# Score products of two heads in two halves of the array's rows, with two-bank score tiles and one shared bank for projections and values

## The chip, the cores and the metric

The kernel runs on one core of a Trainium2 chip. The metric is the device time in microseconds of one execution, taken as the median of several runs; lower is better. The engines are named as in the profile: PE is TensorE's matmul queue, PEld its weight loads, DVE VectorE, ACT ScalarE, POOL GpSimd, SP SyncE, which issues the DMAs.

## The reference

One transformer block on x of shape (1, 2048, 512), with 32 heads of 16 and a window of 256 keys, all in fp32:

```python
sa, ca, ga, sb, cb, gb = split(silu(c) @ w_mod)
h = layernorm(x) * (1 + ca) + sa
x = x + ga * A(h, wqkv, wo)        # sliding-window attention
h = layernorm(x) * (1 + cb) + sb
x = x + gb * B(h, w1, w3, w2)      # silu(h@w1) * (h@w3) @ w2, width 1792

# in A:
scores = einsum("bhqd,bhkd->bhqk", q, k) * 16 ** -0.5
mask = (i - j >= 0) & (i - j < 256)
o = softmax(where(mask, scores, -1e9)) @ v
```

## The kernel before, in words

The program has three parts: a prologue (layer norm, modulation, values of all heads into `vS`), attention in 32 units, and the output projection with the feed-forward part. A unit is one group `g` of 4 heads and one block `b` of 512 queries (`g, b = divmod(u, NB)`, line 827 and its like). The 4 heads are two pairs, `a` = 0 and 1, with two heads `h` in each. Precision is kept by splitting fp32 operands into a rounded fp32r part and a remainder, so a product of two split operands takes three matmuls.

*Where the operands lie.* `ringk` holds keys and `ringq` queries, heads of a pair one above the other: head 0 in rows 0 to 47 (16 elements, three rows each for the split products), head 1 in rows 48 to 95. A query column has values in its own head's rows and zeros in the other's, so a product over all rows gives that head's scores alone. Rows 96 and 97 hold the negative maximum (rounded and remainder) in `ringq` and ones in `ringk`.

*The three steps of a unit.* `unit_a` (line 539): 12 matmuls of 128x128x512 project q and k into the bank `pj` (line 546), ACT copies it out twice (lines 554 and 557), POOL makes the remainder (561), and nine DMAs spread the rows into the rings (567, 569). `unit_b` (line 585): for each of 8 blocks of 64 queries and each pair, one matmul of 96 rows, 128 query columns and up to 320 keys gives scores in a bank `mx` (line 595, "bound product" in this text); DVE adds a mask and takes the row's maximum (604). A transpose on PE (610), a copy on ACT (614), the remainder on DVE (`low`, 617) and two DMAs (621) bring the maxima into rows 96 and 97. `unit_c` (line 825): scores again, with keys on the partitions (line 855), in tiles of one bank `st` with four slots of 128 columns. `WAYS` says for each of six tiles of a pair which key block meets which query blocks; one matmul covers both heads, so it has 256 columns for one query block and 512 for two. The diagonal block ("near") and the block at the window's far end ("far") hold complementary triangles. Where both of a key block's triangles are at hand, DVE merges the far one into the near one in PSUM (`copy_predicated`, 882; with no far block a mask is added, 884), ACT takes one exponential (892), and POOL splits the result into the two with zeros (`affine_select`, 865). Elsewhere ACT copies the block out (860), POOL masks it (865), and ACT takes the exponential (876). Then the value products (905): fp32, the probabilities moving, 17 weight columns (16 values and a one for the sum) of each of four heads into its own 32 partitions of the bank `po`; ACT copies `po` out (912), a DMA stores it (915).

*PSUM's eight banks.* `po` 1, `pj` 1, `mx` 3, `st` 3, all from the pool `psA` (lines 470 and 477). The prologue borrows `st` and `mx`; after attention, the planner of the feed-forward part uses all eight by the table `BANKS`.

*The order of the work.* It is written out. In attention each step has a time in the table `X`, in slots of which a unit has 8; steps of all units are sorted by it (line 1017) and issued in that order, each engine keeping it strictly. After the last units, `ORDER`, `ENGS` and `BANKS` give the order, the engine of each either-or step, and the bank of each product; `Y` and `W` order the prologue.

Of the kernel before, what the change touches and what calls it, by code (L numbers as in the profile page):

```python
# [8 lines left out]
F32 = mybir.dt.float32  # L9
# [9 lines left out]
P = 128  # L19
# [12 lines left out]
X = dict(wqk=(-20.0358, -11.9699, -7.5457), pj=(-28.4873, -28.2135, -28.0501, -27.4756, -25.9988, -25.9357,  # L32
         -25.6912, -25.4459, -24.706, -24.0099, -23.5356, -23.4491), ev=(-22.1624, -21.7023), mix=(-19.0403,),
         row=(-17.1032, -19.8185, -17.762, -16.6896, -19.2827, -20.0079, -16.268, -15.1151, -15.9758),
         mx=(-13.3225, -11.4955, -9.6326, -9.2616, -6.3262, -13.4791, -8.3568, -10.0235, -10.5657, -7.528,
         -7.4334, -11.8695, -7.9956, -6.5249, -9.9457, -11.8384), tl=(1.046, 0.61, 1.469, 1.173, 0.247, 0.052,
         0.282, 0.614, 0.93, 0.988, 1.257, 0.446, 0.598, 0.377, 0.675, 0.778), mr=(-5.806, -5.255, -4.853,
         -2.465, -2.209), st=(1.6653, 1.5726, -0.1141, -0.2946, -0.056, 0.9896, 4.7355, 5.3285, 3.1204, 2.6224,
         3.8659, 5.563), cp=(3.438, 88.47, 0, 0, 0, 0, 6.268, 5.867, 0, 0, 0, 0), mg=(0, 0, -0.004, 0, 0.342,
         1.791, 0, 0, 3.411, 0, 4.304, -58.918), sx=(2.609, 61.173, 0, -0.214, 0, -24.164, 4.963, 5.299, 0,  # L40
         2.956, 0, 5.662), ex=(8.23, 2.612, 0.733, 0, 0.811, 2.465, 9.686, 7.995, 4.324, 0, 4.933, 7.046),
         se=(6.102, -41.609, 1.394, 0, 5.111, 3.506, 9.147, 7.859, 9.091, 0, 8.301, 0.234), pv=(10.1765,
         10.1762, 10.1658, 10.1939, 10.1552, 10.1514), o=(14.1458, 19.2797), job=(3.4574, 10.7246, 14.4495),
         raw=-29.903, gate=18.537)
# [4 lines left out]
         0.331, 0.331, 0.331, 0.331, 0.119, 0.331, 0.331), mr=(8.547, 8.884, 8.95, 9.9, 10.016))  # L49
W = dict(m=0.18, s=0.307, a=0.29, t=0.562, p=0.366, vs=1.748, vo=0.433, wq=(-1.444, 1.47, 1.587), wv0=-2.239, wvh=(-0.578, -0.445, -0.399, -0.345), wvl=(-0.193, -0.326, -0.374, -0.317), wp=1, A0=2.112, h0=0.452, h=6.002, hb=6.868, ls=3.035, la=0.875, rf=(-1.1, -0.393, 6.445), v=2, vt=1.562, mr=(-1.837, 1.507), mm=(3.653, 5.841, 7.356, 7.655), ml=(-1.346, 1.651, 2.536, 6.904), A=1.465, At=7.897, B=10.563)  # L50
MODE = 'AB'
MXB = 3
STB = 3
XB = 6
PTB = 15
# [212 lines left out]
def us(t):  # L268
# [7 lines left out]
             job_dma=("SP", 0.5), scores=("PE", 0.19), top=("DVE", 0.5), parts=("DVE", 0.22), turn=("PE", 0.11), cut=("ACT", 0.16),  # L276
             rows=("SP", 0.67), probs=("ACT", 0.49), copy=("ACT", 0.48), merge=("DVE", 0.33), far=("PE", 0.125),
             part=("POOL", 0.73), part1=("POOL", 0.37), values=("PE", 0.43), cut_all=("ACT", 0.48), store=("SP", 0.45))
# [16 lines left out]
    "PPDDPDDDPDDDDPDPDDDDPPPPDPPDDPDPPPPDDPPPPDDDDDDDDDDPDDDPDDDPDDDDDPDPPPPDPDPDDPDDDDDPDDDDDPPPDDPDDPDD"  # L295
    "PPDPPDDDPPDDPDPPDPPDPPDDPPPPPPPPPPDDDPPPPPDDPPDDDPDDDPPPPPPPPPPPPPPPPDDDPPPDDDPPDDDDDDPDPPPDPPPPDDDP"
    "PDDDDPPPPPPDDDPPDDDDPPPPPPDDDPPDDDDPPPPPDPDDPPPPPPDDPPPPPDDDDDDDPPPPPPDDDPPDDDDPPPPPPDDDPPDDDDPPPPPP"
    "DDDPPDDDDPPPPPPDDDPPDDDDPPPPPPDDDPPDDDDPPPPPPDDDPPDDDDPP")
ORDER = (
# [102 lines left out]
BANKS = dict(dn=(  # L402
    "mpmmssosmmmpsomspmommssossmoommspsmmopmmmmsspmssssmomsmommopsmopspmsmsmsmmsssmssosmmmommpmssopssssmm"
    "psmmmmmosmmomsompsmsmsompsms"),
             tp=(
    "somsposm"),
# [1303 lines left out]
```

## Time and profile before

| | |
|---|---|
| median of 3 runs | 919.24 us (918.39 to 919.66) |
| profiled execution | 918.07 us, span 916.3 us |
| PE, PEld busy | 893.5, 726.0 us |
| DVE, ACT, POOL busy | 654.8, 513.6, 555.2 us |
| granted PE clock | 0.996 |

The span starts with the first instruction of the program and ends with the last. A group of instructions is written as: line, engine, operation, tiles (out<-in), shape, count, then the busy time, the mean of one, the idle time before the group, and what ended it. For a matmul "98x256" after "98*128" means 98 rows and 128 columns of weights, and 256 moving columns. Its recorded length holds the pipeline too, so the distance of two starts says better how long it keeps PE.

### The profile page before, as it was taken

What the parts mean: (1) busy time and instruction counts of PE and PEld (TensorE: products, weight loads), DVE (VectorE), ACT (ScalarE), POOL (GpSimd) and SP (SyncE); (2) the same over time, 40 slices, a digit from 0 to 9 for tenths busy, and PEclk for the clock granted to TensorE, in tenths of its full rate; (3) what the DMA queues carried; (4) which work ended last, traced back from release to release, by engine and by line L of the source; (5) the groups of instructions that cost most, each with busy time, mean ns of one, the idle gap of its engine ahead of it and who ended that gap; (6) DMA issues with size and microseconds to landing.
All of it is one profiled execution on the core that took longest, in us unless ns stands there. A gap on an engine that the chain in (4) does not pass through costs nothing.

```text
span 916.3 us, 18353 instructions
## 1 busy us (share of the span) xinstructions
PE 893.5 (98%) x6052; PEld 726.0 (79%) x6052; DVE 654.8 (71%) x1786; ACT 513.6 (56%) x962; POOL 555.2 (61%) x796
## 2 busy tenths in 40 slices
PE   6999999999999999989998999999999999999998
PEld 2688788888888888866776888888888888888886
DVE  7676778788887778786679668758568665565555
ACT  3433777778778777766597834343465334332330
POOL 6211687787888787867676356886569355435220
PEclk9999999999999999998999999999999999999999
DMA  9631456566655655567875677574272423231102
GB/s 330 201 93 36 109 158 171 165 173 171 178 161 165 174 159 156 144 170 220 266 224 184 211 245 247 174 235 145 85 264 65 159 76 104 66 100 43 46 24 93
DMA packets 126083, 141.73 MB, mean 155 GB/s; under 512 B 61090, under 2 KB 73890, under 8 KB 125988
## 3 DMA queue, kind: packets, MB, share of 16 engines
q1 hardware_dynamic: 125268, 139.51, 50.4%
q10 hardware_dynamic: 720, 1.05, 0.4%
q8 instruction: 48, 0.79, 0.4%
q14 instruction: 47, 0.39, 0.1%
HBM read 85.72 MB, written 34.61 MB: 131 GB/s over the span
## 4 chain that ended last, share of the span: by engine, by line
PE 85%; DMA 4%; DVE 4%; ACT 2%; POOL 2%; issue 2%; SPq 0%; ACTq 0%; POOLq 0%; DVEq 0%
PE st L1472 11%; PE mx L1472 10%; PE pj L548 9%; PE st L855 8%; PE po L905 8%; PE mx L595 7%; PE mx L1568 7%; PE st L1568 6%; PE st L759 5%; PE pj L1472 4%; PE po L1472 3%; PE po L1568 2%; PE pj L1568 2%; DMA vS<-in_wmod 1%; POOL pt L865 1%
## 5 line engine op out<-in xcount | busy, mean ns | idle before, releaser
L604 DVE CUSTOM_DVE_ANT_0 junk<-mx,mskq 128x320 bf16<-128x320 f32 (+4 forms) x512 | 216.5, 466 | 55.0 <-PE mx L595 53.0
L865 POOL TENSOR_SCALAR_AFFINE_SELECT pt<-pt 128x256 f32<-128x256 f32 x472 | 184.7, 413 | 65.9 <-ACT pt L892 26.4
L595 PE MATMUL mx<-ringk,ringq 96*128 96x320 f32 (+4 forms) x512 | 149.3, 314 | 1.6 <-DMA ringq<-qk 1.6
L548 PE MATMUL pj<-hT,wq 128*128 128x512 f32 x384 | 140.2, 401 | 0.0
L892 ACT ACTIVATE pt<-st 128x512 f32<-128x512 f32 (+1 forms) x216 | 117.3, 573 | 33.1 <-DVE st L882 27.6
L855 PE MATMUL st<-ringq,ringk 98*128 98x256 f32 (+1 forms) x536 | 128.4, 328 | 3.3 <-DMA ringq<-mT 1.9
L1067 POOL TENSOR_TENSOR w<-w,w 128x512 fp32r<-128x512 f32 (+2 forms) x49 | 85.2, 1754 | 55.9 <-ACT w L1066 55.2
L595 PEld LDWEIGHTS mx<-ringk,ringq 96*128 96x128 f32 x512 | 95.9, 190 | 13.5 <-issue 2.4
L855 PEld LDWEIGHTS st<-ringq,ringk 98*128 98x128 f32 x536 | 88.3, 191 | 13.3 <-issue 2.5
L905 PE MATMUL po<-pt,vS 128*17 128x128 f32 (+1 forms) x2144 | 89.0, 314 | 0.4 <-ACT pt L876 0.4
L548 PEld LDWEIGHTS pj<-hT,wq 128*128 128x128 f32 x384 | 71.6, 190 | 10.3
L905 PEld LDWEIGHTS po<-pt,vS 128*17 128x17 f32 x2144 | 60.8, 98 | 23.1 <-issue 5.1
L882 DVE COPY_PREDICATED st<-later,st 128x256 f32<-128x256 uint8 x152 | 62.0, 426 | 23.3 <-PE st L855 21.3
L1519 POOL TENSOR_TENSOR t<-t,t 128x512 f32<-128x512 f32 x25 | 33.5, 1342 | 65.4 <-DVE t L1507 65.4
L1472 PE MATMUL st<-b,w 128*128 128x512 f32 x270 | 67.0, 390 | 0.2 <-DVE x1a L1573 0.2
L1472 PEld LDWEIGHTS st<-b,w 128*128 128x128 f32 x270 | 50.5, 188 | 11.5 <-DVE x1a L1573 0.7
L876 ACT ACTIVATE pt<-pt 128x512 f32<-128x512 f32 (+1 forms) x96 | 52.6, 587 | 9.6 <-POOL pt L865 9.4
L860 ACT ACTIVATE pt<-st 128x512 f32<-128x512 f32 (+1 forms) x96 | 52.0, 546 | 8.8 <-PE st L855 8.1
L561 POOL TENSOR_TENSOR qk<-qkr,qk 128x512 fp32r<-128x512 f32 x32 | 41.5, 1298 | 20.0 <-ACT qk L557 19.8
L1066 ACT ACTIVATE w<-w 128x512 fp32r<-128x512 f32 (+2 forms) x56 | 42.4, 784 | 18.7 <-DMA w<-wraw 11.4
L1507 DVE TENSOR_TENSOR t<-mx,t 128x512 f32<-128x512 f32 x44 | 30.1, 685 | 29.4 <-ACT t L1514 12.5
L1507 DVE TENSOR_TENSOR t<-st,t 128x512 f32<-128x512 f32 x40 | 27.4, 686 | 26.7 <-ACT g L1495 9.3
(310 smaller groups left out, 1887.0 us busy)
## 6 DMA issues: line engine op xcount, KB each, us to landing
ringq<-qk SPq DMA_DIRECT2D x192, 64.0 KB, 2.1
ringk<-qk SPq DMA_DIRECT2D x96, 128.0 KB, 2.4
o_dr<-os SPq DMA_DIRECT2D x32, 256.0 KB, 2.2
w<-wsum SPq DMA_DIRECT2D x14, 512.0 KB, 4.3
w<-w2g SPq DMA_DIRECT2D x14, 512.0 KB, 3.7
jb<-in_w SPq DMA_DIRECT2D x24, 256.0 KB, 3.7
w<-wraw SPq DMA_DIRECT2D x14, 384.0 KB, 5.7
vS<-in_wmod SPq DMA_DIRECT2D x20, 256.0 KB, 5.0
```

The lines of the kernel that those rows point to most:

```text
L548: nc.tensor.matmul(v["ps"], WQ[g][w][:, n // 3], hTp(i, n // 3, b * BT, BT), start=(n == 0), stop=(n == 3 * KC - 1))
L595: nc.tensor.matmul(v[i][:, :n], both_queries(a, gs), keys(NS, a, (gs + 1) * HP - n, n), start=True, stop=True)
L604: nc.vector.tensor_tensor_reduce(out=junk[:, :n], in0=v[i][:, :n], in1=mskq[:, WK - n:], scale=1.0, scalar=-3e38, op0=ALU.add, op1=ALU.max ...
L855: nc.tensor.matmul(piece(v[a, k], a, k, m), keys(NM, a, kb * P, P), queries(a, 4 * b + q, n), start=new, stop=not new or len(here(a, k)) = ...
L865: nc.gpsimd.affine_select(out=out, in_=in_, **w)
L882: nc.vector.copy_predicated(o, later, block(v[a, fk], a, fk, m))
L892: nc.scalar.activation(o, i, AF.Exp, scale=SCALE)
L905: nc.tensor.matmul(po[32 * i:32 * i + DH + 1, q * P:(q + n) * P], vS[:, 4 * b + j, 4 * g + i], piece(pt_of(a, k), a, k, m)[:, h], start=i ...
L1067: either(lambda e: e.tensor_tensor(out=lo(), in0=src(), in1=hi().bitcast(F32), op=ALU.subtract), 0.85, 0.06 + 0.0024 * n, key, kl + kh, kl ...
L1472: nc.tensor.matmul(ps(bk), WT[s, n][w][:, col], BB[t, k][r], start=start and c == 0, stop=stop and c == 5, skip_group_check=True)
L1507: return nc.vector.tensor_add(o, x, y)
L1568: nc.tensor.matmul(ps(bk), tiles[hk + (h,)][:, i * P:(i + 1) * P], w2_of(last, y, f), start=(m == 0), stop=(m == 5))
```

## The change

- **Rows.** Each head of a pair gets 64 rows of its own (`HP` = 64): head 0 rows 0 to 63, head 1 rows 64 to 127, with the split's three rows interleaved at a stride of 4. The fourth row holds the negative maximum for the first of the 16 elements; all the rings' free rows are filled with zeros (`ringq`) and ones (`ringk`).
- **Score products.** One matmul of 98 rows for both heads becomes two of 64 rows, one for each head, with half the columns.
- **Score tiles.** Six tiles of one bank for each pair become three of two banks, one bank for each head, with four slots of 128 columns; two such tiles in place of three one-bank tiles. `PIECES` gives key block, first query block, count and slot. In each tile a near and a far block of one key block are merged, so there are six merges in a unit (five before); one block in each of the first two tiles is copied, masked and exponentiated by itself.
- **Maxima.** The bound product now reads all 128 rows, the old maximum of the group before among them, so its result is relative to that; a sum `mtb` for each query block is kept on DVE (`add`), rounded to fp32r. The step `low` goes, and one row is written for each head.
- **Banks.** `pj` and `po` become one bank, `pp`; the values write 32 rows of weights' columns for each head (the 17, and 15 more that lie behind them in memory). The prologue gets four banks of its own (`s0`), attention two two-bank tiles, the feed-forward part four single banks (`sd`), from three pools over the same four banks.
- **Tables.** New `X`, `ENGS`, `ORDER` and `BANKS`; the job's buffer is single; `W` is as before. In the new `X` a unit's PE work stands, by slot, in this order: score tile, bound product, projection, 2 bound, 2 projections, score tile, 2 bound, score tile, 2 bound, values, transpose, bound, score tile, 3 bound, score tile, 2 projections, bound, projection, score tile, bound, 2 projections, bound, 2 projections, bound, projection, bound, projection.

```diff
-STB = 3
+STB = 4
-PTB = 15
+PTB = 8
...
-    def queries(a, qb, n):
+    def queries(a, h, qb, n):
         b, i = divmod(qb, 4)
-        return ringq[:NM, b, a, 2 * i:2 * (i + n)].rearrange("p s h t -> p h s t")
+        return ringq[HP * h:HP * h + HP, b, a, 2 * i:2 * (i + n), h]
...
-    def keys(rows, a, lo, n):
-        return ringk[:rows, a, lo:lo + n]
+    def keys(a, h, lo, n):
+        return ringk[HP * h:HP * h + HP, a, lo:lo + n]
...
-                v["ps"] = psA.tile([P, BT], F32, name="pj", bufs=1)
+                v["ps"] = psA.tile([P, BT], F32, name="pp", bufs=1)
...
+        def add():
+            nc.vector.tensor_tensor(out=mtb[b], in0=v["mt"], in1=mtb[b].bitcast(F32), op=ALU.add)
...
-        def low():
-            nc.vector.scalar_tensor_tensor(out=v["mT"][:, 1], in0=v["tp"][:16, :P], scalar=-1.0,
-                                           in1=v["mT"].bitcast(F32)[:, 0], op0=ALU.mult, op1=ALU.subtract)
...
+    psD = psx.enter_context(tc.tile_pool(name="psD", bufs=1, space=PSUM))
+    PIECES = (((0, 0, 3, 0), (3, 3, 1, 3)), ((1, 1, 3, 1), (-2, 0, 1, 0)), ((2, 2, 2, 0), (-1, 0, 2, 2)))
+    NEAR, FAR, ONE = (0, 1, 0), (2, 3, 3), ((3, 0), (0, 1))
+    EXPS = ((0, 2), (1, 2), (0, 3))
...
+        def scores(a, n):
+            v[a, n] = psD.tile([P, 2, 4, P], F32, name="st", bufs=2)
+            does = here(n)
+            for m, (j, q, c, to) in enumerate(does):
+                for h in range(2):
+                    nc.tensor.matmul(v[a, n][:, h, to:to + c], keys(a, h, (4 * b + j) * P, P), queries(a, h, 4 * b + q, c),
+                                     start=m == 0, stop=m == len(does) - 1, skip_group_check=True)
...
+        def probs(a, n):
+            lo, c = EXPS[n]
+            if n == 2 and not b:
+                c = 2
+            nc.scalar.activation(pt_of(a, n)[:, lo:lo + c].rearrange("p n h k -> p h n k"), v[a, n][:, :, lo:lo + c],
+                                 AF.Exp, scale=SCALE)
...
+        def values_of(n):
+            if "po" not in v:
+                v["po"] = psA.tile([P, BT], F32, name="pp", bufs=1)
+            for j, q, c, at_ in here(n):
+                for i in range(4):
+                    nc.tensor.matmul(v["po"][32 * i:32 * i + 32, q * P:(q + c) * P],
+                                     vflat[:, at_v(4 * b + j, 4 * g + i):at_v(4 * b + j, 4 * g + i) + 32],
+                                     pt_of(i // 2, n)[:, at_:at_ + c, i % 2], start=i not in first, stop=False,
+                                     skip_group_check=True)
+                    first.append(i)
```

More of the change, by code (lines that the diff above doesn't have):

```diff
@@ L275 @@
 KINDS = dict(product=("PE", 0.235), mix=("POOL", 1.25), qk_rows=("SP", 0.65), out=("ACT", 0.5), job=("POOL", 2.0),
-             job_dma=("SP", 0.5), scores=("PE", 0.19), top=("DVE", 0.5), parts=("DVE", 0.22), turn=("PE", 0.11), cut=("ACT", 0.16),
+             job_dma=("SP", 0.5), scores=("PE", 0.28), top=("DVE", 0.5), parts=("DVE", 0.22), turn=("PE", 0.11), cut=("ACT", 0.16),
              rows=("SP", 0.67), probs=("ACT", 0.49), copy=("ACT", 0.48), merge=("DVE", 0.33), far=("PE", 0.125),
-             part=("POOL", 0.73), part1=("POOL", 0.37), values=("PE", 0.43), cut_all=("ACT", 0.48), store=("SP", 0.45))
+             part=("POOL", 0.73), part1=("POOL", 0.37), values=("PE", 0.85), cut_all=("ACT", 0.48), store=("SP", 0.45))
 NPE = 3
@@ L865, in window, with merge @@
             nc.gpsimd.affine_select(out=out, in_=in_, **w)
[L867 to L882 removed]
+        def merge(a, n):
+            o = v[a, n][:, :, NEAR[n]]
+            if n < 2 or b:
+                nc.vector.copy_predicated(o, later, v[a, n][:, :, FAR[n]])
@@ L900, in values_of @@
-        def values_of(k):
-            for a in range(2):
-                for m, (j, q, n) in enumerate(here(a, k)):
-                    for h in range(2):
-                        i = 2 * a + h
-                        nc.tensor.matmul(po[32 * i:32 * i + DH + 1, q * P:(q + n) * P], vS[:, 4 * b + j, 4 * g + i],
-                                         piece(pt_of(a, k), a, k, m)[:, h], start=i not in first, stop=False,
-                                         skip_group_check=True)
-                        first.append(i)
+        def probs(a, n):
[4 more added lines that the diff above has]
+                                 AF.Exp, scale=SCALE)
@@ new lines, in part, with copy, mask, masked_probs @@
+        def part(a, n):
+            pt = pt_of(a, n)
+            window(pt[:, FAR[n]], pt[:, NEAR[n]], 1, 0.0)
+            window(pt[:, NEAR[n]], pt[:, NEAR[n]], 0, 0.0)
+        def copy(a, n):
+            i = ONE[n][0]
+            nc.scalar.activation(pt_of(a, n)[:, i], v[a, n][:, :, i], AF.Copy)
+        def mask(a, n):
+            i, far = ONE[n]
+            window(pt_of(a, n)[:, i], pt_of(a, n)[:, i], far, NEG)
+        def masked_probs(a, n):
+            o = pt_of(a, n)[:, ONE[n][0]]
+            nc.scalar.activation(o, o, AF.Exp, scale=SCALE)
@@ L920, in unit_c @@
         for a in range(2):
-            for k in range(6):
-                i = 6 * a + k
-                does = here(a, k)
-                for m in range(len(does)):
-                    put("sx" if m else "st", i, "scores" if does[m][2] == 2 else "far", scores, a, k, m)
-                if not does or k == 3:
-                    continue
-                if k == 0 or k == 1 and len(WAYS[MODE[a]][k]) == 2:
-                    put("cp", i, "copy", copy, a, k)
-                    put("se", i, "part" if len(does) > 1 else "part1", mask, a, k)
-                    put("ex", i, "probs", masked_probs, a, k)
-                else:
-                    if k in FAR[MODE[a]]:
-                        put("mg", i, "merge", merge, a, k)
-                        if here(a, FAR[MODE[a]][k][0]):
-                            put("se", i, "part", part, a, k)
-                    put("ex", i, "probs", probs, a, k)
-        for k in range(6):
-            if here(0, k) + here(1, k):
-                put("pv", k, "values", values_of, k)
+            for n in range(3):
+                i = 3 * a + n
+                put("st", i, "scores", scores, a, n)
+                put("mg", i, "merge", merge, a, n)
+                put("ex", i, "probs", probs, a, n)
+                if n < 2 or b:
+                    put("se", i, "part", part, a, n)
+                if n == 0 or n == 1 and b:
+                    put("cp", i, "copy", copy, a, n)
+                    put("s2", i, "part1", mask, a, n)
+                    put("e2", i, "probs", masked_probs, a, n)
+        for n in range(3):
+            put("pv", n, "values", values_of, n)
         at(t0 + X["o"][0], out, "cut_all")
@@ L1021, in block_kernel, with singles, take @@
     fixed = [(us(t), fn, *KINDS[kind]) for t, _, fn, kind in last]
-    names = [("st", STB)] * 3 + [("mx", MXB)] * 3 + [("pj", 1), ("po", 1)]
-    free = [end - 1.0] * 3 + [us(8 * (NU - 1) + X["mr"][1]) + 0.4] * 3 + [0.0, end]
+    names = [("sd", STB)] * 4 + [("mx", MXB)] * 3 + [("pp", 1)]
+    free = [end - 1.0] * 4 + [us(8 * (NU - 1) + X["mr"][1]) + 0.4] * 3 + [end]
     urgent = [us(t) for t, _, _, kind in last if kind in ("rows", "qk_rows")]
     ids = {-1 - o[1]: o[2] for o in last}
-    sch = Sched(free, lambda i: psA.tile([P, BT], F32, name=names[i][0], bufs=names[i][1]), fixed, urgent)
     pools = {"a1": a1}
+    def singles():
+        psx.close()
+        pools["sd"] = ctx.enter_context(tc.tile_pool(name="psE", bufs=1, space=PSUM))
+    def take(i):
+        if i < STB and "sd" not in pools:
+            singles()
+        pool = pools["sd"] if i < STB else psA
+        return pool.tile([P, BT], F32, name=names[i][0], bufs=names[i][1])
+    sch = Sched(free, take, fixed, urgent)
     def ps(b):
@@ L1657, in block_kernel @@
             for b in o.bank:
-                b.tile = (sch.take, dict(s=0, m=3, p=6, o=7)[BANKS[b.use][b.n]])
+                b.tile = (sch.take, dict(s=0, m=4, p=7)[BANKS[b.use][b.n]])
     else:
```

160 lines of the change are left out of this document (57 added, 103 removed), and 202 rows, old and new, of the table ORDER.

## The prediction

> **What bounds the kernel now.** I read the page first: its engine line and the chain that ended last.
>
> ```profile
> span 916.3 us, 18353 instructions
> PE 893.5 (98%) x6052; PEld 726.0 (79%) x6052; DVE 654.8 (71%) x1786; ACT 513.6 (56%) x962; POOL 555.2 (61%) x796
> ...
> PE 85%; DMA 4%; DVE 4%; ACT 2%; POOL 2%; issue 2%; SPq 0%; ACTq 0%; POOLq 0%; DVEq 0%
> ```
>
> PE is busy for 98% and is 85% of the chain. The profiled execution took 918.07 us, 1.8 us more than its span; the median of the three timed runs, 919.24, lies 1.2 us above it. I make the sum in span time and add its result to the median.
>
> A mean over the span hides stages, so next I took three windows: attention in its steady state, its end, and the feed-forward part. After that I asked for PE's waits in the first window, and for the transpose of the maxima (line 610), which occurs once in each unit.
>
> ```profile
> 150.00:400.00 250.00, 249.82 (x2643) 211.04 (x2633) 201.47 (x895) 192.97 (x399) 201.12 (x425) 1.00 0.59 164
> 400.00:500.00 100.00, 91.19 (x619) 67.33 (x619) 75.54 (x171) 71.68 (x141) 68.83 (x86) 0.97 0.73 217
> 500.00:916.00 416.00, 412.01 (x1831) 340.46 (x1830) 270.04 (x369) 171.54 (x273) 214.85 (x156) 1.00 0.41 133
> ...
> PE mx L595 <- DMA ringq<-qk: 0.2, 1, 0.2
> ...
> L610 PE MATMUL mx<-ident,mt x23: 276/277/280, 150.2 to 384.8; 128*16 128x128 f32 x23
> ```
>
> Columns of the windows: stretch, length, then PE, PEld, DVE, ACT, POOL. In the first window PE waited 0.2 us in 250. So a nanosecond taken from PE there is a nanosecond of the kernel, until another engine fills up. The 23 transposes have 22 periods between 150.2 and 384.8, so a unit takes 10.66 us. DVE has 201.47/250 x 10.66 = 8.59 us of work in a unit, POOL 8.58, ACT 8.23. The slack before the next engine binds is about 2 us a unit. The last window holds no score product; its tables change but not its products, and I cost it at nothing, +-1 us.
>
> "Busy" counts each matmul's pipeline as well, so I price products by the distance from one start to the next. The timeline of PE alone, around one unit's value products:
>
> ```profile
> 310.25 0.30 PE L905 MATMUL po<-pt,vS 128*17 128x128 f32 x4
> 310.48 0.28 PE L610 MATMUL mx<-ident,mt 128*16 128x128 f32 x1
> 310.51 0.39 PE L595 MATMUL mx<-ringk,ringq 96*128 96x320 f32 x1
> 310.74 0.28 PE L855 MATMUL st<-ringq,ringk 98*128 98x256 f32 x1
> 310.86 0.31 PE L595 MATMUL mx<-ringk,ringq 96*128 96x320 f32 x1
> ...
> 316.76 0.40 PE L548 MATMUL pj<-hT,wq 128*128 128x512 f32 x1
> 317.00 0.31 PE L595 MATMUL mx<-ringk,ringq 96*128 96x320 f32 x1
> 317.15 0.40 PE L548 MATMUL pj<-hT,wq 128*128 128x512 f32 x1
> ...
> 317.54 0.40 PE L855 MATMUL st<-ringq,ringk 98*128 98x512 f32 x1
> 317.78 0.31 PE L595 MATMUL mx<-ringk,ringq 96*128 96x320 f32 x1
> ...
> 318.28 0.31 PE L595 MATMUL mx<-ringk,ringq 96*128 96x320 f32 x1
> 318.52 2.15 PE L905 MATMUL po<-pt,vS 128*17 128x256 f32 x52
> ```
>
> A projection of 512 columns occupies PE for 0.24 us (316.76 to 317.00), a bound product of 320 for 0.15 (317.00 to 317.15), a score product of 256 for 0.12 (310.74 to 310.86) and of 512 for 0.24 (317.54 to 317.78). Going between products of 96, 98 and 128 rows costs nothing. At the values it is different: the bound product before them holds PE for 0.24 (318.28 to 318.52), 0.09 too much.
>
> **Part by part: the score products.** Their groups, over the whole run, by shape, and the value products of the unit above:
>
> ```profile
> L855 PE MATMUL st<-ringq,ringk 98*128 98x256 f32 x352 | 74.4, 290 | 2.5 <-DMA ringq<-mT 1.9 <-ACT pt L892 0.7
> L855 PE MATMUL st<-ringq,ringk 98*128 98x512 f32 x184 | 68.6, 403 | 0.8 <-ACT pt L892 0.8
> ...
> L905 PE MATMUL po<-pt,vS x52: 272/273/391, 318.5 to 320.4; 128*17 128x128 f32 x32, 128*17 128x256 f32 x20
> ```
>
> Now: 352 x 0.12 + 184 x 0.24 = 86.4 us of PE. The change makes 704 products in 352 pairs (24 units with 6 pieces for each of 2 head pairs, 8 first units with 4). The columns are as many as before, but the two products of a pair lie in different halves of the rows and write different banks. If a pair runs side by side, its time is that of one product, and 43.2 us go. If not, nothing goes. No pair of row halves is in this trace. The nearest row is the value products: the 52 above are 13 groups of four heads in four 32-column strips, 8 groups of 128 columns and 5 of 256, or 18 steps of 128. Their starts reach from 318.5 to 320.4, 0.11 us a step, a quarter of what they would take one after the other. So products in separate parts of the array do overlap here, fully, and I take the 43.2. The Trainium skill, "TensorE: Matmul & The Clock Gate", section "Measured speedup vs the span model", has a measured speedup of 3.07 for four row strips; if two strips kept the same share (an estimate, 1.53), about 30 us would go instead, and my sum would end near 903.
>
> **Going between tilings.** All six score tiles of a unit stand alone in the new table, each with full-height products on both sides: 192 tiles, 384 borders. What a border costs is the dispute of this prediction. The low end is zero, as between 96, 98 and 128 rows. The high end is the border of the values: 0.09 on the way in; on the way out the last group of four starts at 310.25 and the next product at 310.48, 0.23, or 0.12 over a step; then the first 128-column weights are not there ahead, and the bound product from 310.51 to 310.74 takes 0.23 instead of 0.15, 0.08 more. In, out and 0.08 for the weights each way are 0.37 us a tile. I take zero, since the row that keeps all 128 columns and varies only the rows is nearer than the one that narrows the columns to 17; the other end is a rival below.
>
> **One bank for q/k and values.** Now a projection waits for two copies of ACT, then the values take the bank, then a third copy, then the next projection.
>
> ```profile
> 318.27 0.58 ACT L554 ACTIVATE qkr<-pj 128x512 f32<-128x512 f32 x1
> 318.75 0.59 ACT L557 ACTIVATE qk<-pj 128x512 fp32r<-128x512 f32 x1
> ...
> 320.92 0.27 ACT L614 ACTIVATE mT<-mx 16x128 fp32r<-16x128 f32 x1 [0.82 <-PE mx L610]
> ...
> 324.39 0.59 ACT L912 ACTIVATE os<-po 128x512 f32<-128x512 f32 x1
> ```
>
> The pair of copies takes 1.07 us (318.27 to 319.34), and starts only when the last projection's record ends, 0.40 after its start: 1.47 from start to free. In the new table two score tiles and four bound products stand between: 0.24 + 2 x 0.24 + 4 x 0.15 = 1.32. PE is late by about 0.2 a unit, all of PE's work queued behind it. On the other side the copy of 0.59 (and the small one of 0.27 ahead of it) has two tiles and four bound products as cover, 1.1 us: nothing, or 0.1. I take 0.2 x 32 = 6 us; its bounds are 0 (the copies start at once, and PE is slower there than I think) and 10.
>
> **Two score tiles in flight instead of three.** Per unit six two-bank tiles replace twelve one-bank tiles. Five of six have 2 us of PE work or more until their buffer is wanted again. The tile of the second pair's middle piece has only about 1.6 (tile, three bound products, three projections and again a bound one), while its own chain is merge, exp and a copy:
>
> ```profile
> L882 DVE COPY_PREDICATED st<-later,st 128x256 f32<-128x256 uint8 x152 | 62.0, 426 | 23.3 <-PE st L855 21.3
> L892 ACT ACTIVATE pt<-st 128x512 f32<-128x512 f32 x184 | 107.4, 601 | 33.1 <-DVE st L882 27.6
> L892 ACT ACTIVATE pt<-st 128x256 f32<-128x256 f32 x32 | 13.1, 409 | 0.0
> L617 DVE SCALAR_TENSOR_TENSOR mT<-mx,mT 16x128 fp32r<-16x128 f32 x26 | 7.1, 272 | 1.5 <-ACT mT L614 1.5
> ```
>
> 0.43 + 0.60 + 0.41 and the product's own 0.40 make 1.84, so PE waits about 0.25: 8 us over 32 units, with 0 and 16 as bounds (DVE or ACT may be ahead of their order or behind it).
>
> **Other engines.** DVE gets a sixth merge in a unit, +0.43, and the add of 16 columns in place of the low part (272 ns; I take the add as between nothing and as long): 8.75 to 9.0 of the new 9.75. POOL keeps 16 windows a unit (8 a pair, as before). ACT copies and exponentiates 5,632 columns where it had 6,400, in 14 instructions for 13: not more. None becomes the bound, but DVE is at 92%. The value products take as many steps, with 32 weight columns for 17: nothing, as their steps are set by 128 moving columns. The maxima's two DMAs stay two, with half the bytes, on the same queue; the nine of q and k only change their stride. The fill of the ring's rows with ones is as long, since its columns are the same, and stands in the prologue, well ahead of the transfers that now write over it. The end of attention (91.19 of 100 us) has one free bank less while the last values hold the shared one: -4 to +4, I take 0.
>
> Sum: -43.2 + 6 + 8 = -29 us. From 919.2: **890 us**, own range 876 (nothing given back) to 908 (pairs at 1.53 or waits at their bounds).
>
> **Rivals.** *The border costs what it costs at the values.* Place: both sides of each score tile. Price 0.37 x 192 = 71 us against 43 saved; PE has so much idle at the borders that the two waits vanish. 919 + 28 = 947; without the exposed weights, 0.21 a tile, it is 40 - 43: 916. It decides from 0.225 us a tile. For it: the value border stands in each unit, and it is the only change of tiling in the trace. The rule of the Trainium skill, "TensorEngine Tiling (Array Packing)", section "Key Properties", speaks for this rival: changing the tiling mode drains the engine, changing the tile does not; by it the time would be near 947, and the trace agrees for columns and shows nothing for rows. Against it: the free steps among 96, 98 and 128 rows, though these may all be one tiling.
>
> *The pairs run one after the other*, so the change does not do what it says. The columns are unchanged, the 168 further instructions have no visible fixed part (0.12 for 256, 0.24 for 512), and the waits find more cover: 919, from 914 to 930.
>
> *DVE sets the pace.* Its 9.0 us fill a unit only so far, since each of its maxima waits for a bound product and each bound product for a buffer that a maximum frees. If it comes no further than 88% (halfway from today's 81% to 95%, my estimate), the period is 10.2 and the time 919 - 0.46 x 32 = 904. For it: three buffers for 16 bound products a unit stay as they are, and DVE's order is fixed. Against it: in the first window PE never waited for it.
>
> **How the numbers follow.** The forecast has a chance of 0.46, the border 0.31, pairs in series 0.12, DVE 0.11. A measurement of this kernel can tell about 0.2% (1.8 us). Faster takes the forecast, DVE and little of the others: 0.57. Same: 0.06, of the series case and of a border near its deciding point. Slower: 0.37. Both signs hold much, so the range reaches from 876, the forecast's low end, over the border's likely value to 948; what it leaves out are dearer borders.
>
> **What would show it.** Right: the two products of a pair start within some 10 ns, the next instruction follows a 384-column pair after about 0.18, the unit's period is about 9.75 and PE shows short waits for ACT ahead of the values. Wrong: the product after a score tile starts 0.1 or more late and its weight load is recorded with it and not ahead of it (border); or a pair's second product starts a whole product later (series); or DVE is busy for over 97% of the window (DVE).

## Result and the profile after

| kernel | median of the runs | profiled span | clock |
|---|---|---|---|
| before, beside it | 919.45 us (918.39 to 920.83, 4 runs) | 916.3 us | 0.996 |
| after | 947.56 us (947.30 to 947.96, 4 runs) | 945.7 us | 0.995 |

The change makes the kernel slower: ratio 1.0305, 95% interval 1.0287 to 1.0323, or 28 us. The forecast was 890 us, with 876 to 948 as its range. The time is near that of the first rival, the one with the border at the value products' price, which had been worked out as 947; how much of that is luck stands in the part on why. Two runs of the experiments that lay above the others of their kernel (2271 us with full rows, 1016 with both products in the same half) are left out of the medians below.

The engine line and the chain of the page after, and PE's waits between 100 and 440 us:

```profile
span 945.7 us, 17339 instructions
PE 923.2 (98%) x5484; PEld 679.7 (72%) x5484; DVE 673.9 (71%) x1826; ACT 500.7 (53%) x970; POOL 546.2 (58%) x784
...
PE 91%; DVE 4%; POOL 1%; issue 1%; ACT 1%; DMA 1%; SPq 0%; DVEq 0%; POOLq 0%; ACTq 0%
```

```profile
PE mx L594 <- DVE mt L603: 1.4, 3, 0.7
PE st L847 <- ACT pt L866: 0.3, 1, 0.3
```

PE still sets the pace: it waits for other engines 1.7 us in 340. It does 568 matmuls fewer (168 score products more, 736 value products fewer) and is busy 30 us longer. So the time is inside PE's own work, and busy time does not show where: a projection's record is 0.40 us long whether the next product starts 0.23 us after it or, as further down, 0.33. The unit's period shows in which part it is. The transposes of the maxima, one in each unit, and the windows of attention's steady state and of its end:

```profile
L612 PE MATMUL mx<-ident,mtb x22: 276/277/278, 155.1 to 397.1; 128*16 128x128 f32 x22
```

```profile
150.00:400.00 250.00, 250.00 (x2072) 162.46 (x2072) 198.28 (x849) 171.01 (x376) 187.60 (x390) 1.00 0.57 152
400.00:500.00 100.00, 93.55 (x656) 61.81 (x652) 76.68 (x219) 67.58 (x141) 71.58 (x115) 0.98 0.78 217
```

22 transposes have 21 periods in 242.0 us: 11.52 us a unit, where it was 10.66 and the forecast 9.75. That is 0.86 more a unit, 27.5 us over 32. DVE did 198.28 us of work in 250. Over a period of 11.52 that is 9.14 us a unit, where it was 8.59; its share fell only because the units became longer.

The first products of the feed-forward part, and a group that reads the tile `wo`, in the kernel before and in the kernel after (behind the count: shortest, median and longest record in ns; the two numbers around "to" are the first and last start):

```profile
L1472 PE MATMUL st<-b,w x270: 388/389/500, 485.9 to 860.2; 128*128 128x512 f32 x135
...
L1472 PE MATMUL mx<-b,wo x132: 389/389/393, 506.9 to 880.6; 128*128 128x512 f32 x132
```

```profile
L1462 PE MATMUL sd<-b,w x324: 387/389/477, 511.4 to 888.7; 128*128 128x512 f32 x162
...
L1462 PE MATMUL mx<-b,wo x120: 390/393/505, 532.3 to 909.6; 128*128 128x512 f32 x120
```

By its start the kernel is 25.5 us late (511.4 against 485.9). From there to the end of the span it was 430.4 us and is 434.3: 3.9 more, in a part whose products are the same. These two numbers, 25.5 and 3.9, are the 29.4 us between the spans.

**What a score tile does to PE.** The timeline of PE in short windows shows one start after the other. In a row "x2" are the two products of a pair, whose starts lie within 0.01:

```profile
300.16 0.40 PE L547 MATMUL pp<-hT,wq 128*128 128x512 f32 x1
300.49 0.39 PE L847 MATMUL st<-ringq,ringk 64*128 64x256 f32 x2
...
300.71 0.28 PE L847 MATMUL st<-ringq,ringk 64*128 64x256 f32 x2
300.92 0.41 PE L594 MATMUL mx<-ringk,ringq 128*128 128x320 f32 x1
...
301.17 0.31 PE L594 MATMUL mx<-ringk,ringq 128*128 128x320 f32 x1
301.41 0.44 PE L847 MATMUL st<-ringq,ringk 64*128 64x384 f32 x2
...
301.69 0.22 PE L847 MATMUL st<-ringq,ringk 64*128 64x128 f32 x2
301.85 0.41 PE L594 MATMUL mx<-ringk,ringq 128*128 128x320 f32 x1
```

The pairs overlap: both start together, and a pair costs the time of one. But each tile is paid for at four places. A projection usually takes 0.23 (the median in this window), and from 300.16 to 300.49 it is 0.33: 0.10 on the way in. The first pair of 256 columns should take the 0.12 of one product and takes 0.22 (300.49 to 300.71): 0.10. The second takes 0.21 to the next product: 0.09 on the way out. And that bound product takes 0.25 instead of 0.15 (300.92 to 301.17): 0.10. In sum 0.39 us. The tile of 384 and 128 columns behind it repeats it: 301.17 to 301.41 is 0.09 over 0.15, 0.28 for the pair of 384 is 0.11 over 0.17, 0.16 for the pair of 128 is 0.10 over 0.06. (That a pair has the length of one product shows in the difference of the two first pairs: 128 columns more for each head add 0.06 us, as much as 128 columns of one product.) Over 144 tiles the medians, worked out in the same way from the distances of starts, are 92, 104, 90 and 104 ns, together 390. The weight loads of the first of the two tiles go with the two terms of 104; the first row is from the kernel before, the load for the score product that starts at 317.54:

```profile
317.39 0.19 PEld L855 LDWEIGHTS st<-ringq,ringk 98*128 98x128 f32 x1
...
300.49 0.30 PEld L847 LDWEIGHTS st<-ringq,ringk 64*128 64x128 f32 x4 [0.37 <-issue]
300.92 0.30 PEld L594 LDWEIGHTS mx<-ringk,ringq 128*128 128x128 f32 x2
```

In the kernel before, the load starts 0.15 us ahead of its product. After each border it starts with its product (300.49 and 300.92). I read this as an array that is emptied, then loaded, then used, on each side; the trace shows the order of the records, not the array itself.

Weight loads of score tiles are also put down to waits for ACT, from 150 to 400 us (total, times, longest):

```profile
PEld st L847 <- ACT pt L866: 6.2, 21, 0.4
PEld st L847 <- ACT qkr L553: 4.2, 22, 0.2
```

A score tile that waits until ACT frees its buffer is what the prediction had costed at 8 us; no load of a projection stands among the waits of this window, where the shared bank was to cost 6. What waits there are lie inside the border: from 100 to 440 us the median way in is 0.08 us at tiles whose load is put down to L866 and 0.09 at those put down to L553, and it is 0.09 at tiles whose load waits for nothing that the profile shows.

### The profile page after: what moved, and what is told of

Read it like the earlier page. It is cut to its first block, busy times and chain, and to the rows that moved or that the text cites. A ratio compares the mean times of both kernels' runs of the same rounds, so it can differ in the third digit from the quotient of the medians.

```text
span 945.7 us, 17339 instructions
## 1 busy us (share of the span) xinstructions
PE 923.2 (98%) x5484; PEld 679.7 (72%) x5484; DVE 673.9 (71%) x1826; ACT 500.7 (53%) x970; POOL 546.2 (58%) x784
## 4 chain that ended last, share of the span: by engine, by line
PE 91%; DVE 4%; POOL 1%; issue 1%; ACT 1%; DMA 1%; SPq 0%; DVEq 0%; POOLq 0%; ACTq 0%
PE sd L1462 14%; PE mx L1462 11%; PE mx L594 11%; PE pp L547 10%; PE pp L891 8%; PE st L847 8%; PE sd L1558 7%; PE mx L1558 7%; PE s L758 5%; PE pp L1462 4%; PE pp L1558 3%; PE s L736 1%; PE mx L612 1%; PE mx L1203 1%; DMA w<-wsum 1%
## 5 line engine op out<-in xcount | busy, mean ns | idle before, releaser
L866 ACT ACTIVATE pt<-st 128x512 f32<-128x512 f32 (+1 forms) x192 | 124.6, 650 | 55.5 <-DVE st L858 41.9
L594 PE MATMUL mx<-ringk,ringq 128*128 128x320 f32 (+4 forms) x512 | 148.8, 339 | 1.4 <-DVE mt L603 1.4
L547 PE MATMUL pp<-hT,wq 128*128 128x512 f32 x384 | 133.4, 404 | 0.0
L594 PEld LDWEIGHTS mx<-ringk,ringq 128*128 128x128 f32 x512 | 88.0, 188 | 31.5 <-DVE mt L603 3.0
L847 PE MATMUL st<-ringq,ringk 64*128 64x384 f32 (+1 forms) x704 | 93.6, 337 | 1.2 <-ACT pt L866 1.2
L891 PE MATMUL pp<-pt,vS 128*32 128x384 f32 (+2 forms) x1408 | 88.2, 390 | 1.1 <-ACT pt L884 0.6
L847 PEld LDWEIGHTS st<-ringq,ringk 64*128 64x128 f32 x704 | 53.7, 185 | 45.5 <-issue 21.3
L1462 PE MATMUL sd<-b,w 128*128 128x512 f32 x324 | 80.0, 390 | 0.0
L547 PEld LDWEIGHTS pp<-hT,wq 128*128 128x128 f32 x384 | 66.5, 188 | 10.6 <-DVE wq L536 0.4
L1462 PEld LDWEIGHTS sd<-b,w 128*128 128x128 f32 x324 | 60.8, 188 | 12.9
L876 ACT ACTIVATE pt<-st 128x256 f32<-128x256 f32 x112 | 42.7, 381 | 25.5 <-DVE st L858 20.8
L1462 PE MATMUL mx<-b,w 128*128 128x512 f32 x198 | 49.8, 390 | 0.0
```

The source lines that it names most:

```text
L547: nc.tensor.matmul(v["ps"], WQ[g][w][:, n // 3], hTp(i, n // 3, b * BT, BT), start=(n == 0), stop=(n == 3 * KC - 1))
L594: nc.tensor.matmul(v[i][:, :n], both_queries(a, gs), ringk[:, a, (gs + 1) * HP - n:(gs + 1) * HP], start=True, stop=True)
L847: nc.tensor.matmul(v[a, n][:, h, to:to + c], keys(a, h, (4 * b + j) * P, P), queries(a, h, 4 * b + q, c), start=m == 0, stop=m == len(does ...
L866: nc.scalar.activation(pt_of(a, n)[:, lo:lo + c].rearrange("p n h k -> p h n k"), v[a, n][:, :, lo:lo + c], AF.Exp, scale=SCALE)
L891: nc.tensor.matmul(v["po"][32 * i:32 * i + 32, q * P:(q + c) * P], vflat[:, at_v(4 * b + j, 4 * g + i):at_v(4 * b + j, 4 * g + i) + 32], p ...
L1462: nc.tensor.matmul(ps(bk), WT[s, n][w][:, col], BB[t, k][r], start=start and c == 0, stop=stop and c == 5, skip_group_check=True)
```

## The experiments

My theory was now the border: going from products over 128 rows to products over 64 and back costs PE about 0.39 us a visit, 192 visits. The rivals were that the pairs do not pay (split heads cost as much as they bring), and that the waits for the shared bank and the two score tiles were the loss. In the diffs, the change's kernel is the base except where it is said.

**The score products over all 128 rows again**, everything else of the change kept. The other head's rows of a query column are zero, so the results stay.

```diff
-        return ringq[HP * h:HP * h + HP, b, a, 2 * i:2 * (i + n), h]
+        return ringq[:, b, a, 2 * i:2 * (i + n), h]
...
-        return ringk[HP * h:HP * h + HP, a, lo:lo + n]
+        return ringk[:, a, lo:lo + n]
```

> The changed kernel with one thing undone: each head's score product reads all 128 rows (the other head's query rows are zeros), so no product is of half height; tiles, banks and order stay. Border theory: a tile costs PE 0.63 us now and would cost 4.4 ns + 0.449 ns a column for each of its products, 0.48 us, so 0.15 x 192 = 29 us go, to about 918; the starts of a pair lie a whole product apart, and weights are recorded ahead of their products again. Rival (the two tiles in flight, the shared bank or the new order cost the time): the products take longer than a pair did, no wait goes, and the time stays at 947 or rises.

Measured: 935.54 us, ratio to before 1.0182 (1.0162 to 1.0203). The period and a tile, again in short windows:

```profile
L612 PE MATMUL mx<-ident,mtb x23: 276/277/278, 154.4 to 396.8; 128*16 128x128 f32 x23
```

```profile
300.02 0.41 PE L547 MATMUL pp<-hT,wq 128*128 128x512 f32 x1
300.27 0.34 PE L847 MATMUL st<-ringq,ringk 128*128 128x384 f32 x1
...
300.69 0.28 PE L847 MATMUL st<-ringq,ringk 128*128 128x128 f32 x1
300.80 0.24 PE L594 MATMUL mx<-ringk,ringq 128*128 128x64 f32 x1
```

It is faster than the change without any overlap: the period is 11.02 (242.4 over 22), 0.50 less, and ahead of the tile nothing is lost but 0.02 (300.02 to 300.27). So the border is worth more than the overlap, as the theory has it. But it came to 936 and not to 918. One cause is in the rows: the second product of 128 columns holds PE for 0.11 us (300.69 to 300.80), twice its 0.06. Two products with 128 columns each need two weight loads, and by the terms of 104 ns above a load of 128 columns takes about 0.1 us, longer than the product. One product for both heads had one load. So splitting the heads costs something even with no border: the period is 0.36 above that of the kernel before, 11.5 us over 32 units, although this difference also holds whatever else the change moves. The feed-forward part's 4 us stand in the 936 too.

**First one head's products, then the other's.** I meant to keep the borders and take the overlap away.

```diff
-            for m, (j, q, c, to) in enumerate(does):
-                for h in range(2):
+            for h in range(2):
+                for m, (j, q, c, to) in enumerate(does):
```

> The changed kernel with each tile's products in another order: both pieces of head 0, then both of head 1, so that only the second piece of head 0 and the first of head 1 can lie side by side. The borders are as many. If the pairs' overlap is worth what the starts say, a tile of 3+1 blocks takes 160 + 53 + 160 ns of streaming instead of 213, one of 2+2 blocks 320 instead of 213: about 0.14 us x 192 = 27 us more, about 974. If the overlap were worth nothing on the chip, 947.

Measured: 950.67 us, ratio 1.0339 (1.0306 to 1.0373), nearly the change's own, and not the expected 974. The trace says why. A tile's four products stand in the program as 384 and 128 columns of head 0, then 384 and 128 of head 1; the rows are what PE was running by 296.145 and what by 296.605:

```profile
296.14 0.45 PE L847 MATMUL st<-ringq,ringk 64*128 64x384 f32 x2
...
296.42 0.23 PE L847 MATMUL st<-ringq,ringk 64*128 64x128 f32 x2
```

The two products of 384 columns start together, the first and the third of the program; the second, of 128, starts 0.28 later with the fourth. A product in one row half overtook one of the other half that stands ahead of it in the program, so the edit had not removed the overlap. It tells nothing of the border.

**Both products of a pair in the same half.** Both use head 0's rows; head 1's scores are left out (head 0's stand in their place), and columns, tiles and borders stay.

```diff
-                    ... keys(a, h, (4 * b + j) * P, P), queries(a, h, 4 * b + q, c),
+                    ... keys(a, 0, (4 * b + j) * P, P), queries(a, 0, 4 * b + q, c),
```

> The changed kernel in which both products of a pair use head 0's rows (head 1's scores are left out, head 0's stand in both banks): borders, tiles, banks and order as in the changed kernel, but two products in one half of the rows can't lie side by side. If the pairs' overlap is worth what their starts say, a tile costs 0.24 us more, 192 x 0.24 = 46 us, about 993. If pairs do not overlap in truth, 947.

Measured: 1002.83 us, ratio 1.0910 (1.0876 to 1.0945). The last row is the window behind attention's steady state, with the granted clock as the third number from its end:

```profile
L612 PE MATMUL mx<-ident,mtb x19: 277/277/278, 154.9 to 388.3; 128*16 128x128 f32 x19
```

```profile
301.08 0.44 PE L847 MATMUL st<-ringq,ringk 64*128 64x384 f32 x1
...
301.36 0.40 PE L847 MATMUL st<-ringq,ringk 64*128 64x384 f32 x2
```

```profile
480.00:520.00 40.00, 39.01 (x244) 23.75 (x234) 20.33 (x52) 21.52 (x48) 23.90 (x45) 0.70 0.57 172
```

The second product starts 0.28 after the first instead of together with it. The period is 12.97 (233.4 over 18), 1.45 above the change's, so the overlap is worth 1.45 us a unit, 46 us over 32. The forecast had 43.2. A little of the 1.45 is not overlap: the second of two products of 128 columns in one half shows its weight load, as with full rows. By time the edit cost 55 us and not 46: most of the rest falls where the clock of the row above was 0.70, and the period does not hold it. This edit takes away what the one before could not.

Two of these kernels differ in the border alone: this one has borders and no overlap, the one with full rows has neither. Their periods are 12.97 and 11.02, so a unit's six borders cost 1.95 us, 0.325 a visit. That is less than the 0.39 of the starts, since part of what a border takes (a weight load that is not hidden) is paid with full rows as well.

**The border alone, in the kernel before.** Six small products a unit, each of 16 columns, behind bound products, into a free part of their bank; nothing uses the results. Once over 64 rows, once over 96.

```diff
+            if i in (1, 4, 6, 9, 11, 14):
+                nc.tensor.matmul(v[i][:, 384:400], ringk[:64, a, ...], ringq[:64, b, a, 0, 0, :16],
+                                 start=True, stop=True, skip_group_check=True)
```

> The kernel before, with six small products of 64 rows added in each unit behind six of its bound products, into unused columns of their bank (16 moving columns, 128 weight columns; the outputs are not used). Border theory: each costs PE a drain on the way in (0.09), its weights (0.10), a drain on the way out (0.09) and the weights of the next product (0.10), 0.39 us with its own few ns: 192 x 0.39 = 75 us on top of 919, about 994. Rival (going to 64 rows is free and only the small product's weights count): the same as with 96 rows, 919 to 935.

> The control of the run with 64 rows: the same six small products in each unit, over 96 rows as the bound products. No border by either theory: each adds a weight load that is at most as long as the 0.10 us of the exposed one, less what lies beside other products, so 0 to 20 us on top of 919.

Measured: 979.92 us over 64 rows, ratio 1.0665 (1.0649 to 1.0680), and 933.33 over 96, ratio 1.0152 (1.0133 to 1.0171). For 192 products that is 0.32 us and 0.08 us each. A place with 64 rows:

```profile
300.01 0.40 PE L548 MATMUL pj<-hT,wq 128*128 128x512 f32 x1
300.24 0.31 PE L595 MATMUL mx<-ringk,ringq 96*128 96x320 f32 x1
300.48 0.27 PE L598 MATMUL mx<-ringq,ringk 64*128 64x16 f32 x1
300.68 0.50 PE L548 MATMUL pj<-hT,wq 128*128 128x512 f32 x1
301.02 0.31 PE L595 MATMUL mx<-ringk,ringq 96*128 96x320 f32 x1
```

The bound product takes 0.24 instead of 0.15, the 16 columns take 0.20, the projection behind them 0.34 instead of 0.24: 0.39 us, the same terms as at a score tile. A place with 96 rows:

```profile
301.40 0.32 PE L595 MATMUL mx<-ringk,ringq 96*128 96x320 f32 x1
301.55 0.17 PE L598 MATMUL mx<-ringq,ringk 96*128 96x16 f32 x1
301.58 0.42 PE L595 MATMUL mx<-ringk,ringq 96*128 96x320 f32 x2
```

Here nothing is lost on the way in (0.15 for the bound product), the 16 columns take 0.03, and in the median the product behind takes 0.08 more than usual, which I read as the small product's own weight load. The 0.24 us between the two kinds, by their times, is the change of rows by itself. The theory had asked for about 0.39 by time and got 0.32; what hid the rest I did not trace.

**Fewer borders.** Score tiles next to each other in twos, for the units below 28 (the second of a pair has only the first's border); and the same table with products over all rows, as a control that has the grouping but no border.

```diff
+XG = {("st", 5): 0.0199, ..., ("st", 4): 2.0978, ..., ("st", 0): 4.2973, ...}
...
-            at(t0 + X[name][i], lambda: fn(*y), kind)
+            at(t0 + (XG.get((name, i), X[name][i]) if u < NU - 4 else X[name][i]), lambda: fn(*y), kind)
```

> The changed kernel with the six score tiles of a unit issued in three pairs of neighbours, in the same sequence and with the same two buffers (units 0 to 27; merges, exponentials and copies moved up with them). Border theory: three tiles of a unit lose their borders, 84 x 0.39 = 33 us, so about 915, less what PE waits for the buffers, which would show as waits for ACT. Rival (buffers and order): tiles back to back press the two buffers harder, so it stays at 947 or gets slower.

> Both edits: tiles in neighbouring pairs and all products over 128 rows. It is the control of the order alone: there are no borders to save, so by the border theory it is within 5 us of the run with full rows alone (about 918), plus what PE waits for the buffers; if the order were what helps the neighbouring tiles, it would gain the same 33 us here.

Measured: 939.55 us, ratio 1.0241 (1.0200 to 1.0281), and the control 954.50, ratio 1.0394 (1.0374 to 1.0413). Removing 3 of 6 visits in 28 units gave 8.0 us (947.56 - 939.55), not 33 (84 x 0.39). But in the control the same grouping cost 19.0 us (954.50 - 935.54). Against it the 84 borders are worth 27.0 us, 0.32 each, as in the kernel before. What the grouping costs is in the waits of the weight loads, first with the tiles in twos, then in the control, from 150 to 400 us (total, times, longest):

```profile
PEld mx L597 <- DVE mt L606: 13.6, 62, 0.3
PEld mx L597 <- ACT mT L619: 7.4, 22, 0.4
```

```profile
PEld mx L597 <- DVE mt L606: 13.2, 53, 0.4
PEld mx L597 <- ACT mT L619: 7.1, 21, 0.4
```

In the change itself no weight load waits for either in this window. Bound products, pushed together by the grouped tiles, seem to run into DVE's maxima and their three buffers. I tried two more tables, which set the tiles beside the value products, where a border is paid anyway: four tiles in twos around them, and one tile on each side of them with the rest alone.

```diff
+XG = {("st", 5): 0.0199, ..., ("st", 1): 3.1, ("st", 4): 3.11, ..., ("st", 3): 3.76, ("st", 0): 3.761, ...}
```

> The changed kernel with the tiles in neighbouring pairs again (units 0 to 27), but one pair stands right ahead of the value products and one behind the first bound product after them, and the merges and exponentials are placed so that the maxima on DVE are not put off. Border theory: of 12 borders of score tiles in a unit, 5 are left that the values did not have anyway, 7 x 0.195 x 28 = 38 us go, to about 909, plus what PE still waits for buffers (0 to 15 us). Rival (the order is what the grouping hurts): it stays above 935.

```diff
+XG = {("st", 1): 3.25, ("mg", 1): 3.28, ("st", 4): 3.27, ("st", 5): 1.5, ("st", 3): 3.95}
```

> The changed kernel with one score tile moved right ahead of the value products and one right behind them (units 0 to 27; two other tiles are shifted by one bound product so that no four bound products stand in a row after the values). Border theory: of a unit's borders between full height and half height two fall away, as the values' own borders now serve the tiles: 2 x 0.195 x 28 = 11 us less, about 937, plus what PE waits for maxima. If a border to the values costs more than one to full height, less than that. Rival (order, not borders): no gain, 947 or more.

Measured: 948.01 us, ratio 1.0318 (1.0302 to 1.0334), and 941.52, ratio 1.0239 (1.0222 to 1.0257). In the first, the weight loads' wait for DVE took the gain; the row is from 150 to 400 us, about 22 units:

```profile
PEld mx L596 <- DVE mt L605: 33.3, 104, 0.6
```

In the second the period fell by 0.19 and the time by 6 us:

```profile
L613 PE MATMUL mx<-ident,mtb x22: 276/277/279, 156.5 to 394.4; 128*16 128x128 f32 x22
```

The borders had been expected to give back 0.39 us a unit; by the distances of starts they gave back 0.3 to 0.4, and new waits took about half of that. So the second effect of the forecast, waits for buffers, exists, but only once the borders no longer cover it. None of the tables came near 919.

**The feed-forward part.** Its products are the same, and yet 3.9 us were lost. In the trace the products that read the tiles named `wo`, `o`, `wq` and `qk` (names that this part uses again) had become longer, those that read `w` had not: 389 to 393 ns for `wo` in the two rows further up. In the compiled kernels the first group had moved: the change shrinks a filler tile, `gapB`, from 120 columns to 24, and some tiles ahead of it, so that `wo0` begins at byte 157184 of a partition before (307 x 512) and at 158592 after (384 bytes beyond a multiple of 512). I gave the change the old filler, and the kernel before the new one.

```diff
-                    slot("gapB", F32, (P, 24))
+                    slot("gapB", F32, (P, 120))
```

> The kernel after, with the filler tile gapB at 120 columns as in the kernel before (24 in the change), so that the tiles of the feed-forward part lie at multiples of 512 bytes of SBUF again and not 384 bytes off; nothing else differs. If the place of the operands sets the feed-forward cadence (231 ns a product after, 227 before), the 1848 products go back to about 227 ns: 4 ns x 1848 = 7 us less at most, of which the change's feed-forward part lost 4.2; I expect 940 to 944 us. If the cadence comes from the new order and banks of that part, nothing moves: 947 to 948 us. Attention's unit period stays at 11.50 us in both.

> The kernel before, with the filler tile gapB at 24 columns as in the kernel after (120 in the kernel before), which moves the feed-forward part's tiles 384 bytes off the multiples of 512; nothing else differs. If the place sets the cadence, the feed-forward products go from 227 to about 231 ns and the time rises by 4 to 7 us, to 923 to 926 us. If order and banks set it, 919 us. Attention's unit period stays at 10.65 us in both.

Measured: the change with 120 columns 939.58 us, ratio 1.0212 (1.0189 to 1.0235); the kernel before with 24 columns 927.58, ratio 1.0087 (1.0071 to 1.0102). That is 8.0 us less and 8.2 more, from the place of some tiles and nothing else. Products started between 520 and 900 us, in brackets; before, before with 24, after, after with 120:

```profile
520.00:900.00 380.00, 379.75 (x1682) 314.00 (x1682) 248.14 (x337) 154.44 (x247) 207.39 (x149) 1.00 0.40 130
```

```profile
520.00:900.00 380.00, 379.72 (x1651) 309.05 (x1651) 241.80 (x327) 155.42 (x248) 206.39 (x149) 1.00 0.41 131
```

```profile
520.00:900.00 380.00, 380.00 (x1663) 309.87 (x1662) 249.10 (x340) 164.43 (x263) 210.43 (x152) 1.00 0.42 138
```

```profile
520.00:900.00 380.00, 379.47 (x1687) 313.13 (x1686) 253.67 (x343) 163.96 (x262) 212.40 (x153) 1.00 0.41 136
```

And in each of the two new kernels the group of `mx` and `wo` of the rows further up, which the filler moved:

```profile
L1472 PE MATMUL mx<-b,wo x132: 390/393/404, 509.3 to 889.8; 128*128 128x512 f32 x132
```

```profile
L1462 PE MATMUL mx<-b,wo x120: 387/389/499, 531.1 to 902.9; 128*128 128x512 f32 x120
```

380 us hold 1682 products at the old place and 1651 at the new (225.9 and 230.2 ns each), in the change 1687 and 1663 (225.3 and 228.5). The record of one follows: 393 ns off the multiple, 389 on it. The starts of the part in these two kernels:

```profile
L1472 PE MATMUL st<-b,w x270: 387/389/501, 488.3 to 868.9; 128*128 128x512 f32 x135
```

```profile
L1462 PE MATMUL sd<-b,w x324: 387/389/496, 510.2 to 882.5; 128*128 128x512 f32 x162
```

Their spans are 926.3 and 938.2 us, so the part takes 438.0 and 428.0, where it took 430.4 in the kernel before and 434.3 in the change. So the 3.9 us seem to be two things: the place costs the change 6.3 (434.3 - 428.0), and at the old place its new order and banks are 2.4 better than those before (430.4 - 428.0). The second is not clear of noise: each span is one execution, and runs of the change with 120 columns lie between 936.0 and 941.4. Which property of the place counts, I did not separate.

## Why the prediction was wrong, step by step

- **What bounds the kernel** held. PE sets the pace after the change as before, and a nanosecond on it is one of the kernel.
- **The pairs overlap: right.** Starts lie within 0.01 us, and same-half products cost 1.45 us a unit, 46 over 32 units, where the step had 43.2. The serial rival falls. But the row it was read from could not show it: a step of the values took 0.11 us for four products of 128 columns, where a score product of 128 columns takes 0.06, and nothing in the trace before gives the price of one value product alone, so "a quarter" and "fully" were guesses that came true. The estimate of 1.53 from the Trainium skill, "TensorE: Matmul & The Clock Gate", section "Measured speedup vs the span model", was too low for two strips here: 128 more columns in both heads cost 0.06 us, as much as in one, a factor of 2.
- **The border: this is the step that failed.** The prediction said "I take zero, since the row that keeps all 128 columns and varies only the rows is nearer than the one that narrows the columns to 17". The runs show 0.39 us a visit at score tiles, and 0.39 in the trace or 0.32 by time for a small product of 64 rows alone, while 96 rows cost no way in. So 96, 98 and 128 rows act as one tiling, as the text itself held possible, and that row was no evidence on the question. The other end, 0.37, was within 0.02 of the trace. The deciding point was 0.225, and every measured price, 0.32 to 0.39, lies above it. With the rule of the Trainium skill, "TensorEngine Tiling (Array Packing)", section "Key Properties", that a switch of mode drains the engine, the trace agrees for rows too: 0.09 to 0.10 us on the way in, 0.09 on the way out. The weights on either side, 0.10 each, are as dear.
- **Two products in place of one, at nothing: too low.** The prediction saw no fixed part in the further products. With full rows the period was 0.36 us a unit above the kernel before, 11.5 us over 32, and the rows show a part of it, the second weight load of a tile's pieces of 128 columns.
- **One bank and two score tiles, 6 and 8 us: neither came on top.** PE waited 1.7 us in 340, and the loads' waits for ACT lie inside the borders, as the first rival had said. That waits return as borders go, the grouped tables show.
- **The last window at nothing, +-1: too low by 3.9.** The products are the same, but I did not look where their operands lie.
- **DVE as the pace setter** did not come up: it was busy for 79% of the first window. Its work in a unit, 9.14 us, is a little above the 9.0 that the prediction allowed. With the tiles in twos, waits for its maxima appear.
- **The range.** Its inner end of 908 does not follow from the bounds named for it: pairs at 1.53 give 903, and both waits at their bounds 902.

The sum with the terms of the starts: 192 x 0.39 = 75 us for borders, 46 back from the overlap, 4 in the feed-forward part: 33 us, against 28 by the medians. The sum by periods is nearer: in a unit 0.36 for two products in place of one, 1.95 for the borders and 1.45 back, 0.86 together, or 27.5 us over 32 units; with the feed-forward part 31.4, where the spans differ by 29.4. The last 2 us lie in the first and last units, where the steady period doesn't hold (attention came out 25.5 us late and not 27.5); I did not trace them.

So the rival's 947 was right in its cause and partly lucky in its number: its borders were 9 us too dear (71 for 62), and its sum had neither the 11.5 us of the second products nor the 3.9 of the feed-forward part.

Whether the change's idea pays with fewer borders stays open in part. The overlap of 1.45 us a unit and a border of 0.39 mean that at most three visits a unit (1.17) leave a gain in the score products themselves. Against the kernel before, the overlap leaves 1.45 - 0.36 = 1.09, and three visits at 0.325 (0.98) use nearly all of it. The table that I tried with three visits paid it back in waits for DVE. A table with other buffers for the bound products was not tried.

## What to carry to other kernels

Splitting a product into row halves pays only where one visit holds much work: here a visit costs 0.32 to 0.39 us, and overlapping a tile's pairs saves about 0.24. When two rows of a trace disagree on a price, ask whether the reassuring row crosses the same border at all; three sizes between which nothing is paid (96, 98 and 128 rows) say nothing on the step to a fourth. And after an edit that changes the size of any tile, compare the length of the products that were not edited.

## What the runs showed of the hardware

- A visit to 64-row products among 128-row ones costs 0.09 us in, 0.10 for weights not loaded ahead, 0.09 out and 0.10 for weights again, by the distances of starts; by the periods of the kernels with full rows and with both products in the same half it is 0.325.
- Products in different row halves didn't keep the program's order in their starts: a tile's third product started with the first, 0.28 us ahead of the second.
- A product of 128 columns with weights of its own, behind another such, takes 0.11 us instead of 0.06, about as long as the load of 128 weight columns at a border (0.10).
- Products of 512 columns in the feed-forward part took longer with operands that begin 384 bytes off a multiple of 512 in SBUF: 393 against 389 ns in the record, and 228.5 to 230.2 against 225.3 to 225.9 ns a product over 380 us. The place alone moved this kernel by 8 us either way; what in the place does it is open. The projections of attention don't show it: their `hT` moved by the same 384 bytes, and their distance of starts did not grow (0.24 before, 0.23 after).
